# Attention scores in Float32r for three of four batches, a shorter MAX8 for the 32nd score, and batch 1 sent through the first MoE in two groups

## The chip, the cores and the metric

The kernel runs on one core of a Trainium2 chip. The metric is the device time of one execution in microseconds (us). One execution of the kernel before was profiled; its trace has the instructions of TensorE (PE, with its weight loads as PEld), VectorE (DVE), ScalarE (ACT), GpSimd (POOL) and SyncE (SP, which here issues DMAs only), and the DMAs.

## What is computed

Three stages follow each other: attention that keeps the 32 largest scores of each row, a gated MLP ("first MoE", one dense expert), and a layer with 8 experts of which each token uses one ("second MoE").

```python
# q, k, v: 4 batches x 8 heads x 576 rows x 64
scores = scale * np.matmul(q, k.transpose(0, 1, 3, 2))
kth = np.partition(scores, -32, axis=-1)[..., -32:-31]
scores = np.where(scores >= kth, scores, -1e9)
attn = softmax(scores); x = attn @ v            # x: 2304 tokens x 512
x = ((x @ w_a) * (x @ w_b)) @ w_out             # first MoE, d_ff 1536
expert_idx = argmax(x @ w_gate)                 # second MoE, 8 experts
out[mask] = gate_w * (relu(x[mask] @ w1[e]) @ w2[e])
```

## The kernel before

The kernel writes its work as a list of operations, each with an engine, an estimated cost, the tiles that it reads and writes, and a position. A planner (`Plan.emit`) simulates the engines with these costs and fixes the order of each engine's instructions: of the operations that are ready it takes the one with the lowest position. On the chip each engine then runs its list in that order, whatever the real times are. All plain loads and stores go through SP's one queue, in order.

Attention works in units: one batch, one pair of heads. A unit loads q, k and v of the two heads (`load_unit`), and turns q and k with PE transposes, which ACT copies out of PSUM (`prep_unit`). The preparation of a unit is placed in the time of the unit before it. Then come tiles of 128 query rows. Two tiles, the two heads of the same rows, make a pair (kind "N"); the last 64 rows of both heads make one tile (kind "M"). `attn_tiles` computes the scores of a pair in two halves of 288 keys. Each half is two matmuls on float32 operands of 64 partitions (L533; each appears as two instructions in the trace, and so a half as x4). ACT copies the half to SBUF (L537). DVE takes the larger (`m`) and the smaller (`n`) of score j and score j + 288 (L545), finds the 32 largest of `m` by four rounds of MAX8 with three MATCH_REPLACE8 between them (L556, L569, L572), and the 8 largest of `n` by one MAX8 (L575). `attn_kth` makes the 32nd largest score of the row out of these with a minimum over two short lists (L585) and a maximum (L587). `attn_out` masks the exponentials with it (L609 on DVE and L611 on POOL, or L615 on DVE alone), transposes the result (L640), and `attn_av` multiplies by v (L661, L665).

There are 144 tiles, 36 for each batch. `GRP` cuts the 576 tokens of a batch into a group of 320 and one of 256. Of batch 0 the tiles of the first group are computed for all four head pairs, go through the first MoE, and then those of the second (`HALVES` holds 0): 8 units. The batches 1, 2 and 3 have four units each, of 9 tiles, and go through the first MoE with both groups at once.

The first MoE of a batch (`moe1`) runs on PE in float32r, with every operand as a high and a low part and three products (L758 for the two input matrices, L788 for the output matrix). Its matmuls have the lowest priority on PE and fill what attention leaves. For each half of d_ff, six weight pieces of 1 MB (`wt<-ws`) are loaded, each used for all groups at hand, then four of 0.75 MB (`wt<-wos`), through three buffers. A piece that is used for both groups is loaded once for both; batch 0 loads every piece once for each group. The weights come as float64 and are first converted, split and stored to DRAM (`conv`, L369 to L418) in 36 steps, which are placed between the tiles of batch 0 and end with the first tiles of batch 1. After each pass through the first MoE a gating step (`gating`, its first matmul is L871) finds each token's expert and scatters the rows to `xsort`, which is filled with empty rows before by eight DMAs of 771 KB (L339). The second MoE follows when all tokens have been gated.

Of the kernel before, what the change touches and what calls it, by code (L numbers as in the profile page):

```python
# [24 lines left out]
def fr(ap):  # L25
    return ap.bitcast(F32)
# [183 lines left out]
def fused_kernel(ctx: ExitStack, tc: tile.TileContext, q, k, v, w_a, w_b, w_out, w_gate, w1, w2, out,  # L210
# [20 lines left out]
    HALVES = opts.get("halves", (0,))  # L231
# [48 lines left out]
    am_t = [cst.tile([128, S], F32, name="am0")]  # L280
    make_identity(nc, am_t[0][:, 0:128])
    nc.vector.tensor_copy(idr, am_t[0][:, 0:128])
    tri = cst.tile([128, 128], F32, name="tri")
# [21 lines left out]
    rr_t = []  # L305
# [15 lines left out]
    for i in range(1):  # L321
        gb_t.append(cst.tile([128, 346], F32, name=f"gb{i}"))
        nc.gpsimd.memset(gb_t[i], 0.0)
    RR = [P_.fixed(t) for t in rr_t]
# [101 lines left out]
    def load_unit(ui, b, p, groups, pos, after=None):  # L426
        u = Rec()
        u.b, u.p, u.first = b, p, ui == 0
# [9 lines left out]
        for nm, src in (("k", k), ("q", q)):  # L438
            z = T(p_at, [128, 10, 64], F32, "raw" + nm, opts.get("raw", 1))
            u.raw[nm] = z  # L440
            a, e, last = u.c if nm == "q" else (0, 4, True)
            for h in range(2):
                load(c_dma(65536 * (e - a)), pos, lambda z=z, h=h, a=a, e=e: z()[:, h + 2 * a:h + 2 * e - 1:2, :],
                     src[b, h0 + h, 0:512, :].rearrange("(p c) d -> p c d", c=4)[:, a:e], [(z, h)])
            if last:
                load(c_dma(65536), pos, lambda z=z: z()[0:64, 8:10, :],
                     src[b, h0:h0 + 2, 512:576, :].rearrange("h s d -> s h d"), [(z, 2)])
# [9 lines left out]
    def prep_unit(u, i, pos, step):  # L457
        u.rr = RR[i % len(RR)]
        u.qT = T(p_at, [128, 640], F32, "qT", 2)
        u.kT = T(p_at, [128, 640], F32, "kT", 2)  # L460
        for ni, (nm, z) in enumerate((("k", u.kT), ("q", u.qT))):
            raw = u.raw[nm]
            p1 = pos + 3 * ni * step
            a, e, last = u.c if nm == "q" else (0, 4, True)
            t = T(p_ps, [128, 512], F32, "pv", 1) if u.first and nm == "q" else T(p_ps, [128, 1024], F32, "tp", 1)
            cut = [(a, e, last)] if not u.first or nm == "q" else [(0, 2, False), (2, 4, True)]
            for a, e, last in cut:

                o = 128 * e if u.first and nm == "q" else 512

                def tr(t=t, raw=raw, a=a, e=e, last=last, o=o):
                    for c in range(a, e):
                        res = nc.tensor.transpose(t()[:, c * 128:(c + 1) * 128],
                                                  raw()[:, 2 * c:2 * c + 2, :].rearrange("p a d -> p (a d)"), idf)
                    if last:
                        res = nc.tensor.transpose(t()[:, o:o + 64], raw()[0:64, 8:10, :].rearrange("p a d -> p (a d)"),
                                                  idf[0:64, 0:64])
                    return res
                P(PE, 110 * (e - a) + 60 * last, p1, tr, r=[raw], w=[(t, a)], act=0)

                def out(t=t, dst=z, a=a, e=e, last=last, o=o, f=64 * (nm == "k")):
                    if last and f:
                        nc.scalar.copy(dst()[:, 0:64], t()[:, 512:S])
                    if last and 128 * e < 512:
                        nc.scalar.copy(dst()[:, 512:S], t()[:, o:o + 64])
                        last = False
                    x, y = 128 * a, S if last else 128 * e
                    return nc.scalar.copy(dst()[:, f + x:f + y], t()[:, x:y])
                u.mark = P(ACT, c_act(128 * (e - a) + 64 * last) + (150 if last and (e < 4 or nm == "k") else 0), p1,
                           out, r=[(t, a)], w=[(z, a)])  # L490

    def new_group(u, g):
# [3 lines left out]
        r.kth = T(p_sml, [128, 5], F32, "kth", 2)  # L496
# [6 lines left out]
    def attn_tiles(lst, r, pos):  # L503
# [8 lines left out]
        if kind == "M":  # L512
            sp = T(p_ps, [128, 2, 512], F32, "sp", 1)

            def score():
                for hh, hf in ((0, 0), (1, 1), (0, 1), (1, 0)):
                    a = slice(64 * hh, 64 * hh + 64)
                    res = nc.tensor.matmul(sp()[a, hf, 0:HS], u.qT()[a, 512:576], u.kT()[a, 64 + hf * HS:64 + (hf + 1) * HS],
                                           start=True, stop=True)
                return res  # L520
            P(PE, 980, pos, score, r=[u.qT, u.kT], w=[sp], label=f"score{u.b}")
# [3 lines left out]
        else:  # L525
            for hf in range(2):
                sp = T(p_ps, [128, 2, 512], F32, "sp", 1)

                def score(hf=hf, sp=sp):
                    for h in range(2):  # L530

                        a, k0 = slice(64 * h, 64 * h + 64), 0 if h else 64
                        res = nc.tensor.matmul(sp()[:, h, 0:HS], u.qT()[a, c * 128:(c + 1) * 128],  # L533
                                               u.kT()[a, k0 + hf * HS:k0 + (hf + 1) * HS], start=True, stop=True)
                    return res
                P(PE, 510, pos, score, r=[u.qT, u.kT], w=[sp], label=f"score{u.b}")
# [30 lines left out]
        for x in range(1, 4):  # L567
            for h, (i, j, kind, _, c) in enumerate(lst):
# [5 lines left out]
                if x == 1:  # L574
                    P(DVE, c_dve(HS), pos + 5.0 * h + 0.5, lambda h=h, j=j: nc.vector.max(  # L575
                        out=kt(j, 40, 48), in_=n()[:, h]), r=[(n, h)], w=[KT(j, 5)])
        return res

    def attn_kth(r, j0, j1, pos):
        def kt(a, b):  # L580
            return r.kt()[:, j0:j1, a:b]

        def KT(x):
# [936 lines left out]
```

## Time and profile before

| | |
|---|---|
| median of 3 runs | 1248.7 us (1246.32 to 1249.34) |
| the profiled execution | 1250.73 us, its span 1248.9 us |
| mean granted PE clock | 0.944 of full speed |
| PE busy | 1136.4 us, 91% of the span |
| DVE busy | 893.8 us, 72% |
| ACT busy | 741.5 us, 59% |
| POOL busy | 539.2 us, 43% |
| DMA | 208.01 MB, mean 167 GB/s |

The shares are means over stages with different limits: attention and the first MoE overlap, and the second MoE comes alone at the end. A matmul's busy time is longer than the step from one matmul to the next, since matmuls are pipelined, so that costs of PE are read as steps between start times.

### The profile page before, as it was taken

The numbers are of one execution on the slowest core, as the hardware profiler recorded it, in microseconds if no ns is written. First come the engines' busy times: TensorE is split into PE (matmuls) and PEld (weight loads), VectorE is DVE, ScalarE is ACT, GpSimd is POOL, SyncE is SP. The second block draws the span as 40 slices with busy tenths as digits, with TensorE's granted clock in tenths as the row PEclk, the third lists the DMA queues.
The fourth block names the chain that finished last, engine by engine and source line by source line (L and its number), as shares of the span: only waits on it lengthen the run. The fifth ranks groups of instructions, "written<-read, shape, count | busy, mean of one in ns | idle before, by whom it ended". The sixth has DMA issues, their size and how long they took to land.

```text
span 1248.9 us, 22260 instructions
## 1 busy us (share of the span) xinstructions
PE 1136.4 (91%) x7614; PEld 950.9 (76%) x7614; DVE 893.8 (72%) x2574; ACT 741.5 (59%) x1639; POOL 539.2 (43%) x673
## 2 busy tenths in 40 slices
PE   5666587987999999999999999999899999999997
PEld 2333365675687878878878777899899889999996
DVE  6999989999989999989999898901004644444451
ACT  6767677777677776656766665633223545544451
POOL 4766667577554744324544532555334110000011
PEclk9966588898899999999999999999999999999999
DMA  7486566898466554243243322345545645554550
GB/s 232 137 275 186 164 178 188 288 327 264 161 208 200 188 183 131 77 130 131 77 137 100 113 86 104 119 140 202 196 167 179 200 151 171 181 175 145 166 180 28
DMA packets 133375, 208.01 MB, mean 167 GB/s; under 512 B 53075, under 2 KB 95059, under 8 KB 125573
## 3 DMA queue, kind: packets, MB, share of 16 engines
q1 hardware_dynamic: 130037, 197.04, 48.5%
q0 software_dynamic: 3216, 9.46, 2.0%
q8 instruction: 62, 1.02, 0.3%
q14 instruction: 60, 0.49, 0.1%
HBM read 171.82 MB, written 35.25 MB: 166 GB/s over the span
## 4 chain that ended last, share of the span: by engine, by line
PE 62%; DVE 20%; issue 7%; DMA 5%; ACT 3%; POOL 2%; SPq 1%; POOLq 0%; ACTq 0%; DVEq 0%
PE ab L758 20%; PE ab L788 11%; PE sp L533 5%; PE ab L1116 5%; DVE m L569 4%; PE pv L661 4%; DVE kt L572 4%; PE tp L640 3%; PE ms L1165 3%; PE pv L1165 3%; DVE am L609 2%; DVE kt L556 1%; DMA xsort<-rows,pi 1%; DVE am L615 1%; DVE m L545 1%
## 5 line engine op out<-in xcount | busy, mean ns | idle before, releaser
L758 PE MATMUL ab<-xh,wt 128*128 128x320 f32 (+1 forms) x1344 | 311.1, 309 | 3.4 <-ACT sb L743 3.4
L758 PEld LDWEIGHTS ab<-xh,wt 128*128 128x128 f32 x1344 | 228.3, 192 | 30.3 <-issue 22.6
L758 PE MATMUL ab<-xl,wt 128*128 128x320 f32 (+1 forms) x672 | 200.4, 298 | 0.0
L569 DVE MATCH_REPLACE8 m<-kt,m 128x288 f32<-128x288 f32 x432 | 190.6, 447 | 0.0
L572 DVE MAX8 kt<-m 128x8 f32<-128x288 f32 x432 | 184.8, 452 | 0.7
L788 PE MATMUL ab<-gH,wt 128*128 128x320 f32 (+1 forms) x768 | 172.0, 307 | 2.8 <-DMA wt<-wos 2.8
L533 PE MATMUL sp<-kT,qT 64*128 64x288 f32 x512 | 111.2, 514 | 40.5 <-ACT s L537 13.0
L766 POOL TENSOR_TENSOR sa<-sa,sb 128x320 f32<-128x320 f32 (+1 forms) x96 | 80.2, 836 | 149.2 <-ACT sb L743 145.6
L788 PEld LDWEIGHTS ab<-gH,wt 128*128 128x128 f32 x768 | 129.8, 193 | 14.9 <-issue 10.1
L611 POOL TENSOR_TENSOR am<-am,e 128x576 f32<-128x576 f32 x78 | 119.1, 1532 | 31.8 <-DVE am L609 25.7
L758 PEld LDWEIGHTS ab<-xl,wt 128*128 128x128 f32 x672 | 129.2, 192 | 0.0
L1190 POOL DMA_INDIRECT out_dram<-y,ti x23 | 23.0, 999 | 228.0 <-ACT y L1184 213.3
L564 ACT ACTIVATE e<-s,nm 128x576 f32<-128x576 f32 x144 | 109.5, 777 | 16.4 <-POOL nm L559 15.5
L788 PE MATMUL ab<-gT,wt 128*128 128x320 f32 (+1 forms) x384 | 114.8, 299 | 0.0
L640 PE MATMUL tp<-idr,am 128*128 128x128 f32 x512 | 87.9, 307 | 24.7 <-DVE am L615 12.3
L1034 DVE TENSOR_TENSOR wp<-raw,wp 128x1024 fp32r<-128x1024 f32 (+1 forms) x73 | 67.5, 943 | 55.0 <-ACT wp L1033 52.6
L537 ACT COPY s<-sp 128x576 f32<-128x576 f32 x128 | 81.8, 639 | 41.9 <-PE sp L533 31.0
L395 POOL TENSOR_TENSOR gT<-sa,gH 128x320 fp32r<-128x320 f32 (+1 forms) x96 | 82.6, 861 | 39.5 <-ACT gH L394 38.1
L640 PEld LDWEIGHTS tp<-idr,am 128*128 128x128 f32 x512 | 65.7, 157 | 44.4 <-POOL am L611 14.4
L533 PEld LDWEIGHTS sp<-kT,qT 64*128 64x128 f32 x512 | 44.1, 209 | 72.3 <-issue 28.2
L1116 PE MATMUL ab<-xgh,wp 128*128 128x304 f32 (+6 forms) x352 | 89.5, 312 | 1.2 <-DVE gT L1123 0.7
L644 ACT COPY aT<-tp 128x512 f32<-128x512 f32 x128 | 73.4, 586 | 24.6 <-PE tp L640 23.7
(286 smaller groups left out, 2559.6 us busy)
## 6 DMA issues: line engine op xcount, KB each, us to landing
wt<-ws SPq DMA_DIRECT2D x54, 1024.0 KB, 4.8
wt<-wos SPq DMA_DIRECT2D x44, 768.0 KB, 4.6
raw<-in_moe_w_dram SPq DMA_DIRECT2D x64, 512.0 KB, 3.5
xsort<-rows SPq DMA_DIRECT2D x8, 771.0 KB, 10.5
wp<-ws SPq DMA_DIRECT2D x6, 1024.0 KB
rawk<-in_k_dram SPq DMA_DIRECT2D x40, 128.0 KB, 3.6
vt<-in_v_dram SPq DMA_DIRECT2D x20, 256.0 KB, 4.4
gT<-in_moe_w_a_dram SPq DMA_DIRECT2D x8, 512.0 KB
```

The costliest lines, as they stand in the source:

```text
L395: P(POOL, c_pool(cost), pos, lambda: nc.gpsimd.tensor_sub(lo(), src(), fr(hi())), r=rd + wh, w=wl)
L533: res = nc.tensor.matmul(sp()[:, h, 0:HS], u.qT()[a, c * 128:(c + 1) * 128], u.kT()[a, k0 + hf * HS:k0 + (hf + 1) * HS], start=True, stop= ...
L537: P(ACT, c_act(S), pos, lambda hf=hf, sp=sp: nc.scalar.copy(s()[:, :, hf * HS:(hf + 1) * HS], sp()[:, :, 0:HS]), r=[sp], w=[(s, (h, hf)) f ...
L564: P(ACT, c_act(S, True) + 90, pos, lambda h=h, e=e: nc.scalar.activation(e(), s()[:, h], AF.Exp, bias=nm()[:, h], scale=SCALE), r=[(s, (h, ...
L569: P(DVE, c_dve(HS), pos + 5.0 * h, lambda x=x, h=h, j=j: nc.vector.match_replace(out=m()[:, h], in_to_replace=kt(j, 8 * x - 8, 8 * x), in_ ...
L572: P(DVE, c_dve(HS), pos + 5.0 * h, lambda x=x, h=h, j=j: nc.vector.max(out=kt(j, 8 * x, 8 * x + 8), in_=m()[:, h]), r=[(m, h)], w=[KT(j, x)])
L611: P(POOL, c_pool(S), pos, lambda: nc.gpsimd.tensor_mul(am(), am(), e()), r=[e], w=[amk])
L640: res = nc.tensor.transpose(tp()[:, 512 * h + x * 128:512 * h + (x + 1) * 128], z()[:, 640 * h + x * 128:640 * h + (x + 1) * 128], idf)
L758: res = nc.tensor.matmul(pa()[:, 0:n], view()[:, m, wi, ko, :], xv()[:, ko], start=(ko == 0 and x == 0), stop=(ko == KO - 1 and x == 2))
L766: P(POOL, c_pool(n), pos, lambda: nc.gpsimd.tensor_mul(sa()[:, 0:n], sa()[:, 0:n], sb()[:, 0:n]), r=[sb], w=[sa])
L788: res = nc.tensor.matmul(pa()[:, 0:n], wv()[:, wi, f, :], gv()[:, f, :], start=(f == 0 and x == 0), stop=(f == HB - 1 and x == 2))
L1116: res = nc.tensor.matmul(pa()[:, 0:cap], p1[ko]()[:, wi, f * 128:(f + 1) * 128], xv()[:, ko], start=(ko == 0 and i == 0), stop=(ko == KO - ...
```

## The change

1. `HALVES` becomes (0, 1): batch 1 too is computed group by group. It then has 8 units and goes through the first MoE in two passes, with its weight pieces loaded twice and a gating step after each. There are 24 units instead of 20, still with 144 tiles.
2. `FU` is the set of units that keep float32 scores: the first eight, which are those of batch 0. For all others q and k are split into a high and a low float32r part (`hl`: a copy on ACT, a subtraction on POOL), transposed with both parts stacked on 128 partitions, and copied out for each head. For k a second copy with the two parts exchanged (`kS`) is made by two DMAs on SP's queue. A half of a pair's scores is then four float32r matmuls with 128 partitions: q's stack times `kT` and times `kS`, for each head. The rows of kind "M" use eight. q, k and v are loaded whole for each such unit. The planner's cost of a float32 half goes from 510 to 780 ns; that of a float32r half is 490.
3. The 32nd score: the last round of MAX8 on `m` (8 values) and the MAX8 on `n` (8 values) lie side by side, and one MAX8 over these 16 values for each tile replaces L585 and L587. Its 8th value is the 32nd score.
4. The small last transposes of an "M" tile (L624, 64 by 64) become one of 128 by 128 on a tile padded with zeros.

```diff
-    HALVES = opts.get("halves", (0,))
+    HALVES = opts.get("halves", (0, 1))
+    FU = opts.get("fu", range(8))
...
-        u.b, u.p, u.first = b, p, ui == 0
+        u.b, u.p, u.f, u.first = b, p, ui in FU, ui == 0
...
+            load(c_dma(262144), pos, lambda z=z: z()[:, 0:8, :].rearrange("p (h c) d -> p h c d", h=2),
+                 src[b, h0:h0 + 2, 0:512, :].rearrange("h (p c) d -> p h c d", c=4), [(z, 0)])
             for h in range(2):
...
+                load(c_dma(16384), pos, lambda z=z, h=h: z()[64 * h:64 * h + 64, 8, :], src[b, h0 + h, 512:576, :],
+                     [(z, 1 + h)])
...
+        u.qT = T(p_at, [128, 2, 512], F32R, "qT", 2)
+        u.kT = T(p_at, [128, 2, 640], F32R, "kT", 2)
...
+        u.kS = T(p_at, [128, 2, 640], F32R, "kS", opts.get("kS", 2))
+        for ni, nm in enumerate(("k", "q")):
             raw = u.raw[nm]
...
+            p0 = pos + 3 * ni * step
+            hl = T(p_at, [128, 9, 2, 64], F32R, "hl", opts.get("hl", 1))
+            P(ACT, c_act(576, True), p0, lambda raw=raw, hl=hl: nc.scalar.copy(hl()[:, :, 0, :], raw()[:, 0:9, :]),
+              r=[raw], w=[(hl, 0)])
+            P(POOL, c_pool(576), p0, lambda raw=raw, hl=hl: nc.gpsimd.tensor_sub(
+                hl()[:, :, 1, :], raw()[:, 0:9, :], fr(hl()[:, :, 0, :])), r=[raw, (hl, 0)], w=[(hl, 1)])
+            for h in range(2):
+                p1 = p0 + step * (1 + h)
+                t = T(p_ps, [128, 1024], F32R, "tp", 1)
+                lst = [(c, 4 * h + c) for c in range(4)] + ([(4, 8)] if h else [])
+
+                def tr(t=t, lst=lst, hl=hl):
+                    for c, j in lst:
+                        r = nc.tensor.transpose(t()[:, c * 128:(c + 1) * 128],
+                                                hl()[:, j].rearrange("p a d -> p (a d)"), idr)
+                    return r
+                P(PE, 56 * len(lst), p1, tr, r=[hl], w=[t], act=0)
+                if nm == "q":
+                    P(ACT, c_act(512), p1, lambda t=t, h=h: nc.scalar.copy(u.qT()[:, h, :], fr(t()[:, 0:512])),
+                      r=[t], w=[(u.qT, h)])
+                else:
+                    P(ACT, c_act(512), p1, lambda t=t, h=h: nc.scalar.copy(u.kT()[:, h, 64:576], fr(t()[:, 0:512])),
+                      r=[t], w=[(u.kT, h)])
...
+                    for a in range(2):
+                        u.mark = P(SP, c_dma(294912), p1, lambda a=a: nc.sync.dma_start(
+                            fr(u.kS()[64 * a:64 * a + 64]).rearrange("p h c -> p (h c)")[:, 64:],
+                            fr(u.kT()[64 - 64 * a:128 - 64 * a]).rearrange("p h c -> p (h c)")[:, 64:]),
+                          r=[u.kT], w=[(u.kS, a)])
...
+                        for x, kk in enumerate((u.kT(), u.kS())):
+                            res = nc.tensor.matmul(sp()[:, h, 0:HS], u.qT()[:, h, c * 128:(c + 1) * 128], kk[:, h, kc],
+                                                   start=(x == 0), stop=(x == 1))
                     return res
-                P(PE, 510, pos, score, r=[u.qT, u.kT], w=[sp], label=f"score{u.b}")
+                P(PE, 780 if u.f else c_mm(HS, 4), pos, score, r=[u.qT, u.kT] + ([] if u.f else [u.kS]), w=[sp],
+                  label=f"score{u.b}")
...
-                        out=kt(j, 40, 48), in_=n()[:, h]), r=[(n, h)], w=[KT(j, 5)])
+                        out=kt(j, 32, 40), in_=n()[:, h]), r=[(n, h)], w=[KT(j, 4)])
...
-        P(DVE, 77 + 8 * (j1 - j0 - 1), pos, lambda: nc.vector.tensor_tensor(
-            kt(32, 40), r.kt()[:, j0:j1, 30:22:-1], kt(40, 48), op=OP.min), r=KT(2) + KT(3) + KT(5), w=KT(4))
-        P(DVE, 78 + 9 * (j1 - j0 - 1), pos, lambda: nc.vector.tensor_reduce(
-            r.kth()[:, j0:j1], kt(31, 40), axis=AX.X, op=OP.max), r=KT(3) + KT(4), w=[(r.kth, j) for j in range(j0, j1)])
...
+        for j in range(j0, j1):
+            P(DVE, 80, pos, lambda j=j: nc.vector.max(out=r.kt()[:, j, 40:48], in_=r.kt()[:, j, 24:40]),
+              r=[(r.kt, (j, 3)), (r.kt, (j, 4))], w=[(r.kt, (j, 5))])
```

The branch for the units in `FU` is the old code of `load_unit` and `prep_unit`, moved into an `if u.f`.

## Rows read from the trace of the kernel before

**Rows 1.** Busy time by stretch; after POOL: granted PE clock, DMA share, GB/s.

```profile
225.00:350.00 125.00, 110.53 (x682) 83.24 (x680) 119.30 (x354) 90.99 (x207) 76.89 (x85) 0.92 0.79 254
350.00:430.00 80.00, 79.34 (x605) 64.46 (x603) 73.14 (x247) 61.00 (x149) 46.51 (x63) 1.00 0.60 200
430.00:640.00 210.00, 209.82 (x1509) 169.56 (x1510) 193.14 (x627) 140.04 (x322) 97.06 (x131) 1.00 0.38 123
640.00:811.00 171.00, 169.44 (x1216) 136.97 (x1215) 153.53 (x506) 109.02 (x252) 71.64 (x103) 1.00 0.31 107
811.00:975.00 164.00, 158.03 (x1187) 153.84 (x1185) 22.24 (x79) 55.74 (x146) 70.62 (x100) 0.99 0.52 181
```

**Rows 2.** The same view, one stretch of 25 us in the early stage.

```profile
275.00:300.00 25.00, 20.46 (x120) 15.81 (x122) 23.92 (x73) 20.39 (x49) 19.17 (x22) 0.88 0.99 317
```

**Rows 3.** Timeline of SP's issues: start, length, what, count.

```profile
303.87 0.53 SPq L418 DMA_DIRECT2D wos<-gH  x1
...
334.65 3.06 SPq L736 DMA_DIRECT2D wt<-ws  x2
```

**Rows 4.** Chain that ended last, in order of time: start, length, what.

```profile
243.44 1.88 PE pv L661 x16
...
437.73 1.88 PE pv L661 x16
...
805.46 0.44 PE tp L640 x4
...
816.55 1.62 PE ab L758 x12
...
825.50 19.20 PE ab L788 x144
844.69 0.68 PE ms L871 x8
```

**Rows 5.** Timeline of PE: a preparation of k, then an "M" score.

```profile
440.12 0.66 PE L473 MATMUL tp<-idr,rawk 128*128 128x128 f32 x4
...
440.90 1.19 PE L518 MATMUL sp<-kT,qT 64*64 64x288 f32 x8
```

**Rows 6.** Timeline of PE: a score half between two other pieces.

```profile
449.47 0.31 PE L758 MATMUL ab<-xh,wt 128*128 128x320 f32 x1
449.71 0.76 PE L533 MATMUL sp<-kT,qT 64*128 64x288 f32 x4
450.40 0.44 PE L882 MATMUL ms<-idr,rows 128*128 128x128 f32 x2
```

**Rows 7.** Groups by line and shape: busy us, mean ns, idle before.

```profile
L611 POOL TENSOR_TENSOR am<-am,e 128x576 f32<-128x576 f32 x78 | 119.1, 1532 | 31.8 <-DVE am L609 25.7 <-PE sp L518 2.9 <-PE sp L533 2.2
...
L644 ACT COPY aT<-tp 128x512 f32<-128x512 f32 x128 | 73.4, 586 | 24.6 <-PE tp L640 23.7
...
L575 DVE MAX8 kt<-n 128x8 f32<-128x288 f32 x144 | 65.3, 453 | 0.0
...
L585 DVE TENSOR_TENSOR kt<-kt 128x16 f32<-128x16 f32 x64 | 21.3, 334 | 0.1
...
L488 ACT COPY kT<-tp 128x576 f32<-128x576 f32 x19 | 12.3, 648 | 0.0
...
L587 DVE TENSOR_REDUCE kth<-kt 128x2 f32<-128x18 f32 x64 | 10.3, 161 | 0.1
```

**Rows 8.** One line's instructions: shortest, median, longest ns, first and last start.

```profile
L585 DVE TENSOR_TENSOR kt<-kt x80: 144/176/1296, 21.8 to 809.0; 128x16 f32<-128x16 f32 x64, 128x8 f32<-128x8 f32 x16
...
L575 DVE MAX8 kt<-n x144: 435/452/482, 15.5 to 807.6; 128x8 f32<-128x288 f32 x144
...
L615 DVE SCALAR_TENSOR_TENSOR am<-s,kth,e x66: 794/814/1902, 31.0 to 810.7; 128x576 f32<-128x576 f32 x66
```

**Rows 9.** Waits of SP's queue: us in total, times, longest.

```profile
SPq L776 <- PE ab L758: 170.2, 21, 16.2
```

**Rows 10.** The page, DMA issues: count, KB each, us to landing.

```profile
xsort<-rows SPq DMA_DIRECT2D x8, 771.0 KB, 10.5
```

More of the change, by code (lines that the diff above doesn't have):

```diff
@@ L304, in fused_kernel @@
     nc.gpsimd.memset(wg, 0.0)
-    rr_t = []
+    qm_t, rr_t = [], []
+    for i in range(2):
+        qm_t.append(cst.tile([128, 192], F32R, name=f"qm{i}"))
+        nc.gpsimd.memset(fr(qm_t[i]), 0.0)
     for i in range(opts.get("rr", 1)):
@@ L323, in fused_kernel @@
         nc.gpsimd.memset(gb_t[i], 0.0)
+    QM = [P_.fixed(t) for t in qm_t]
     RR = [P_.fixed(t) for t in rr_t]
@@ L457, in prep_unit @@
     def prep_unit(u, i, pos, step):
[L458 to L461, printed above, removed]
-            raw = u.raw[nm]
[L463 to L490, printed above, removed]
@@ new lines, in prep_unit, with tr, out @@
+        u.qm, u.rr = QM[i % 2], RR[i % len(RR)]
+        u.qT = T(p_at, [128, 2, 512], F32R, "qT", 2)
+        u.kT = T(p_at, [128, 2, 640], F32R, "kT", 2)
+        if u.f:
+            u.qv, u.kv = (lambda z=z: fr(z()).rearrange("p h c -> p (h c)")[:, 0:640] for z in (u.qT, u.kT))
+            for ni, (nm, z, dst) in enumerate((("k", u.kT, u.kv), ("q", u.qT, u.qv))):
+                raw = u.raw[nm]
+                p1 = pos + 3 * ni * step
+                a, e, last = u.c if nm == "q" else (0, 4, True)
+                t = T(p_ps, [128, 512], F32, "pv", 1) if u.first and nm == "q" else T(p_ps, [128, 1024], F32, "tp", 1)
+                cut = [(a, e, last)] if not u.first or nm == "q" else [(0, 2, False), (2, 4, True)]
+                for a, e, last in cut:
+                    o = 128 * e if u.first and nm == "q" else 512
+                    def tr(t=t, raw=raw, a=a, e=e, last=last, o=o):
+                        for c in range(a, e):
+                            res = nc.tensor.transpose(t()[:, c * 128:(c + 1) * 128],
+                                                      raw()[:, 2 * c:2 * c + 2, :].rearrange("p a d -> p (a d)"), idf)
+                        if last:
+                            res = nc.tensor.transpose(t()[:, o:o + 64], raw()[0:64, 8:10, :].rearrange("p a d -> p (a d)"),
+                                                      idf[0:64, 0:64])
+                        return res
+                    P(PE, 110 * (e - a) + 60 * last, p1, tr, r=[raw], w=[(t, a)], act=0)
+                    def out(t=t, dst=dst, a=a, e=e, last=last, o=o, f=64 * (nm == "k")):
+                        if last and f:
+                            nc.scalar.copy(dst()[:, 0:64], t()[:, 512:S])
+                        if last and 128 * e < 512:
+                            nc.scalar.copy(dst()[:, 512:S], t()[:, o:o + 64])
+                            last = False
+                        x, y = 128 * a, S if last else 128 * e
+                        return nc.scalar.copy(dst()[:, f + x:f + y], t()[:, x:y])
+                    u.mark = P(ACT, c_act(128 * (e - a) + 64 * last) + (150 if last and (e < 4 or nm == "k") else 0), p1,
+                               out, r=[(t, a)], w=[(z, a)])
+            return
@@ L515, in score @@
             def score():
[L516 to L519, printed above, removed]
-                return res
-            P(PE, 980, pos, score, r=[u.qT, u.kT], w=[sp], label=f"score{u.b}")
+                if u.f:
+                    for hh, hf in ((0, 0), (1, 1), (0, 1), (1, 0)):
+                        a = slice(64 * hh, 64 * hh + 64)
+                        res = nc.tensor.matmul(sp()[a, hf, 0:HS], u.qv()[a, 512:576],
+                                               u.kv()[a, 64 + hf * HS:64 + (hf + 1) * HS], start=True, stop=True)
+                    return res
+                for hf in range(2):
+                    for hh in range(2):
+                        for kk in (u.kT(), u.kS()):
+                            res = nc.tensor.matmul(sp()[:, hf, 0:HS], u.qm()[:, 64 * hh:64 * hh + 128],
+                                                   kk[:, hh, 64 + hf * HS:64 + (hf + 1) * HS],
+                                                   start=(hh == 0 and kk is u.kT()), stop=(hh == 1 and kk is u.kS()))
+                return res
+            P(PE, 980 if u.f else c_mm(HS, 8), pos, score, r=[u.qT, u.kT] if u.f else [u.qm, u.kT, u.kS], w=[sp],
+              label=f"score{u.b}")
             P(ACT, c_act(S), pos, lambda: nc.scalar.copy(
```

57 lines of the change are left out of this document (34 added, 23 removed).

## Prediction

> **What bounds the kernel now.** I read the busy times by stretch first, because the page's shares mix stages. In each row the reader is to compare PE with the length of the stretch. From 225 to 350 us PE works 110.5 of 125 us at a mean clock of 0.92, while DVE is busy 119.3; from 350 to 811 it works 458.6 of 461 us at full clock [rows 1]. So PE is the limit from about 340 us on, and DVE, with 92% there, comes close behind. After 811 us DVE is nearly idle and PE goes on with the first MoE.
>
> Second comes the queue of SP, for where the early stage ends. The last converted piece of the output weights is stored at 303.87 us, and the first weights of batch 0's second group are issued at 334.65 [rows 3]. Until then PE waits for conversions, which DVE, ACT, POOL and the DMAs share with attention; between 275 and 300 us the DMAs are busy 0.99 of the time [rows 2].
>
> Third, the chain that ended last shows what slack attention has. Its last piece ends at 816.55 us; PE then still has batch 2's first MoE to finish, whose gating starts at 844.69 [rows 4]. Batch 3's first MoE begins behind it. So attention may end some 28 us later without harm, and time is saved by shortening PE's list after 340 us, not by shortening DVE's.
>
> **Scores.** A float32 half takes PE 0.80 us: the last matmul before it starts at 449.47, the next would start 0.133 later (144 float32r matmuls of 320 and 256 columns in 19.20 us [rows 4]), and the instruction behind the half starts at 450.40 [rows 6]. Four float32r matmuls of 288 columns, the mean of those two widths, with the same 128 by 128 weights, take 4 x 0.133 = 0.53. The gain is 0.27 for a half; if the gap of about 0.11 us before it stays, it is 0.16. There are 3 batches x 4 head pairs x 4 tile pairs x 2 halves = 96, so 25.6 us, at least 15. An "M" score takes 1.19 us now [rows 5] and 8 x 0.133 = 1.07 then: nothing to speak of.
>
> **Preparation on PE.** k takes 440.90 - 440.12 = 0.78 us [rows 5], q as much, 12 units: 18.7 us. Then it is 18 transposes for each of 16 units, 288 in all. No row has a float32r transpose. Its floor is the 128/288 of 0.133 by columns, 0.06 us; its ceiling the float32 one, 0.44/4 = 0.11 [rows 4]. That gives 17 to 32 us; I take 0.08 for the weight load behind each, 23 us, so +4 (between -2 and +13).
>
> **What of it counts.** PE's list gets 26 - 4 = 22 us shorter (2 to 28). Batch 1's attention runs from 243 to 438 us [rows 4], so half of its 32 halves lie ahead of 340, where PE waits anyway: 4 us of gain is lost there and 2 us of the added transposes are free. A second gating for batch 1 costs PE about 1 us (its first matmuls take 0.68 [rows 4]). Some -19 us remain. The larger transposes of the "M" tile change a fifth of a microsecond 16 times at most, and both ways.
>
> **The 32nd score.** For a pair DVE drops 334 + 161 ns and adds two MAX8 over 16 values. MAX8 over 288 takes 453 [rows 7]; over 16 it lies between nothing and that; nearest in size is the reduction of 18 values, 161. So 495 becomes about 320, on 64 pairs 11 us, at worst a loss of 26. It is DVE time beside PE's full list: after 340 us it is worth nothing, ahead of it, where DVE paces the conversions, 25 pairs x 0.175 = 4 us, of which I count 3.
>
> L585 shows why it is dear: 144 ns at the shortest, 176 median, 1296 at the longest, while MAX8 stays between 435 and 482 [rows 8]. The Trainium skill, "SBUF — State Buffer", section "Who interferes with whom", says that a VectorE instruction with two SBUF inputs and a GpSimd instruction that reads SBUF shut each other out for a whole instruction, and one with a single input does not. The trace agrees, with the spreads just named. By that rule the change takes L585 out of POOL's way, but its 32 new POOL subtractions come in the way of L615 (814 median, 1902 longest [rows 8]); at the price of the wait that L615 has now, for POOL time that grows by a seventh, this gives back some 2 us of DVE, and the sum stays.
>
> **ACT, POOL and DMA.** A unit's ACT work is now two copies of 576 at 0.65 us [rows 7] and one small one, 1.5 us; then two copies of 576 from SBUF (0.65), four of 512 at 0.59 [rows 7], and four small ones at half of that: 4.8. So 16 x 4.8 - 12 x 1.5 = 59 us more on ACT, which is busy 401 of the 586 us from 225 to 811 [rows 1], so 68% becomes 78%. POOL gets 32 subtractions of 576 at 1.5 us [rows 7], 49 us, from 50% to 58%. Neither is a limit by its share. But PE's results wait for ACT in two buffers, each filled again in 12 x 0.133 = 1.6 us, hardly longer than two or three ACT copies in a row. PE stands still 2.4 of the 461 us now; I add 3 us, between 0 and 15.
>
> The second loading of batch 1's weights adds 12 + 6 = 18 MB between 340 and 660 us, where the DMAs are busy 0.4 to 0.6 of the time. Batch 0's second group, loaded in the same one-group way, lets PE work 79.3 of 80 us at 200 GB/s [rows 1]. I cost it at nothing; the cover is that DMA room, and without it each piece would hold PE for the part of 1 MB / 317 GB/s = 3.3 us [rows 2] that exceeds its matmuls (24 x 0.133 = 3.2). Ahead of 340 us there is no room: batch 1 begins two units more in that stretch, each with 0.9 MB from DRAM and 0.6 MB of `kS`, 3 MB or 9 us of full DMAs. If the last conversions stand behind this, PE's full stretch begins up to 9 us later; I take 4, so with DVE's gain of 3 the stretch begins 1 us later.
>
> The split itself gives PE little, since at 340 us it already has a full list; it makes batch 1's first group ready before batch 0's second is through, and so covers the seam at about 445 us.
>
> **Sum.** -19 + 1 + 3 = -15; I keep 2 us more for waits that I have not found, -13. The profiled execution took 1250.7 us, 2.0 more than the median of the runs: 1237.7 there, 1236 for the median.
>
> **Rivals.**
>
> *Late scores (slower).* `kS` is issued on SP, in order, behind weight loads that wait for a free buffer, 21 times, up to 16.2 us [rows 9], and a DMA in the full stretch took 10.5 us to land [rows 10]. Scores wait for it, and DVE for them. For it: a chain of copy, subtraction, transposes, copies and two DMAs where before there were transposes and a copy. Against it: preparation runs a unit ahead, 40 us in batches 2 and 3, though only some 20 in batch 1. Attention has 28 us of slack, less PE's gain of 15, plus DVE's 7 after 340: 20. From a stretch of 20 + 13 = 33 us on, 2 us for each of 16 units, the change loses; at 3 us for each unit it is 48, so 28 past the slack, and 1236 + 28 = 1264.
>
> *ACT becomes the limit of PE's buffers (no change).* At 15 us of waits instead of 3, and transposes at 0.11 (+9 more), the sum is about +8 less 1: 1236 + 12 to 1236 + 20, 1248 to 1256; with one of the two, 1245 to 1248.
>
> *The early stage is filled (a larger gain).* From 225 to 350 us PE loses 14.5 us idle and 8% of clock on the rest, 23 in all [rows 1]. A plan with truer costs may start the full stretch earlier by most of that: 1236 - 17 = 1219. Against it: the conversions still set the stage.
>
> **Chances.** A difference under 0.3%, 4 us, can't be told from none. Forecast (1227 to 1245): 0.50; larger gain: 0.10; no change: 0.16; late scores: 0.24. The no-change case reaches a little over both of its bounds. Faster 0.62, within 0.3% 0.15, slower 0.23. The likeliest case's own range is 1227 to 1245; that for 8 in 10 reaches into the others: 1219 to 1262.
>
> **What would show it.** Right: float32r score halves of about 0.53 us between neighbours on PE; PE full from about 340 us; the gating of batch 2 some 15 us earlier than 844.69; attention's end before 816 us. DVE's new MAX8 near 160 ns with little spread. Wrong: transposes at 0.11 us or more; PE idle behind ACT's copies in the first MoE; DVE waiting for scores at the start of units and the second weights issued well after 334.65; attention ending after the first MoE of batch 2.

## The result: 1.2% slower

| | before | after |
|---|---|---|
| median us (four runs each) | 1247.9 (1246.32 to 1249.34) | 1263.49 (1262.62 to 1263.57) |
| the profiled execution, its span | 1250.73, 1248.9 | 1262.62, 1260.7 |
| mean granted PE clock | 0.944 | 0.939 |
| DMA | 208.0 MB | 240.4 MB |

The ratio is 1.012, 95% interval 1.0105 to 1.0135. The forecast was 1236. The time, and the late attention, are those of the rival "late scores" (1264).

Page of after, busy time of each engine:

```profile
PE 1116.9 (89%) x7790; PEld 990.0 (79%) x7790; DVE 897.8 (71%) x2570; ACT 782.0 (62%) x1764; POOL 578.2 (46%) x707
```

PE is busy 19.5 us less, and the kernel still takes longer. The busy time by stretch (columns as in [rows 1]) says where PE stood still instead:

```profile
225.00:350.00 125.00, 101.50 (x711) 90.09 (x711) 98.29 (x295) 92.81 (x222) 83.74 (x93) 0.92 0.89 286
350.00:430.00 80.00, 74.81 (x594) 67.46 (x591) 57.07 (x185) 59.58 (x146) 48.69 (x61) 0.96 0.77 244
430.00:640.00 210.00, 202.53 (x1560) 183.98 (x1558) 192.33 (x612) 153.75 (x369) 115.47 (x148) 1.00 0.69 226
640.00:811.00 171.00, 162.71 (x1205) 146.41 (x1206) 166.29 (x539) 117.41 (x279) 72.17 (x99) 0.97 0.34 111
```

Against [rows 1], PE's idle time grows from 14.5 to 23.5 us in the first stretch, from 0.7 to 5.2 in the second, from 0.2 to 7.5 in the third and from 1.6 to 8.3 in the fourth: 27.5 us together. The granted clock falls with it: 1.00 from 350 to 811 us before, 0.96 and 0.97 in the second and fourth stretch after. There it drops to the lower of its two levels (1.2 GHz) for a few us at a time, where PE has stood still: from 360 to 370 us PE is busy 7.04 us at a mean clock of 0.67, and 2.9 us of its idle time are in one piece. So a part of PE's busy time in after is work at half the clock. DVE, which sets the pace of attention, is busy 98 us of the first stretch instead of 119, and 57 of the second instead of 73. The DMA share rises from 0.79 to 0.89, from 0.60 to 0.77 and from 0.38 to 0.69.

Waits of DVE in after while batch 1's attention runs (242 to 477 us; us in total, times, longest):

```profile
DVE m L614 <- ACT s L606: 29.2, 9, 8.3
DVE sum L752 <- POOL sum L750: 14.1, 5, 3.5
DVE m L614 <- PE sp L601: 9.3, 3, 7.4
```

The same view of before, from 243 to 440 us:

```profile
DVE m L545 <- ACT s L537: 4.2, 3, 1.6
DVE n L545 <- ACT s L537: 2.5, 4, 0.7
DVE sum L686 <- POOL sum L684: 1.7, 3, 0.8
...
DVE m L545 <- PE sp L533: 1.0, 2, 0.6
```

DVE now waits 12 times, 38.5 us, for the first scores of a pair (5 times, 5.2 us, before), and 14.1 us for sums from POOL (1.7 before). One such wait, timeline of DVE in after (the bracket is the idle time ahead and what ended it):

```profile
307.50 0.19 DVE L752 RECIPROCAL sum<-sum 128x5 f32<-128x5 f32 x1 [3.06 <-POOL sum L750]
316.00 0.76 DVE L614 TENSOR_TENSOR m<-sp,s 128x576 f32<-128x576 f32 x1 [8.31 <-ACT s L606]
```

The chain that ended last, in after, leads to this wait through two transfers:

```profile
274.27 13.61 DMA xsort<-rows
...
293.10 10.26 DMA wt<-wos
303.40 1.97 PE ab L854 x6
...
316.00 0.76 DVE m L614
```

By this chain the scores that DVE waits for stand in PE's list behind matmuls of the first MoE (L854), which start when a weight piece (`wt<-wos`) has landed, and SP issues that piece only after a fill of `xsort` and the loads of a unit. Just ahead of 303 us PE also stands idle 3.3 and 3.4 us for POOL.

So batch 1's attention takes 236 us (its last product with v starts at 477 us) where it took 194 [rows 4]: 42 us more for the same 36 tiles. Batches 2 and 3 win back some of it. PE timeline of after, the ends that answer to 816.55 and 844.69 in [rows 4]:

```profile
641.42 0.64 PE L937 MATMUL ms<-x,wg 128*32 128x256 f32 x8
...
842.39 1.95 PE L727 MATMUL pv<-aT,vt 128*64 128x256 f32 x16
...
854.85 0.75 PE L937 MATMUL ms<-x,wg 128*32 128x320 f32 x8
```

The gating of batch 1's last tokens starts at 641, where before it was 657: there PE's gain is still seen. But that lead is the first MoE's alone, taken while attention fell behind: attention ends at 842 instead of 814 (start of the last product), and batch 2's gating comes at 855 instead of 845. The balance of PE closes: -19.5 of busy time, +20.8 of idle time from 225 to 640 us, +6.7 from 640 to 811 and +3.8 elsewhere make the +11.8 us of the two profiled spans (the medians differ by 15.6).

### The profile page after: what moved, and what is told of

Its sections match the earlier page's. It is cut to its first block, busy times and chain, and to the rows that moved or that the text cites. A ratio compares the mean times of both kernels' runs of the same rounds, so it can differ in the third digit from the quotient of the medians.

```text
span 1260.7 us, 23056 instructions
## 1 busy us (share of the span) xinstructions
PE 1116.9 (89%) x7790; PEld 990.0 (79%) x7790; DVE 897.8 (71%) x2570; ACT 782.0 (62%) x1764; POOL 578.2 (46%) x707
## 4 chain that ended last, share of the span: by engine, by line
PE 45%; DVE 23%; issue 10%; DMA 10%; ACT 6%; POOL 4%; SPq 2%; POOLq 0%; DVEq 0%; ACTq 0%
PE ab L824 13%; PE ab L854 8%; DVE m L638 5%; PE ab L1182 5%; DVE kt L641 4%; PE pv L727 3%; PE sp L601 3%; PE pv L1231 2%; PE tp L706 2%; PE ms L1231 2%; DMA xsort<-rows,pi 2%; DMA wt<-wos 2%; DVE am L674 2%; DVE am L680 2%; DVE kt L625 1%
## 5 line engine op out<-in xcount | busy, mean ns | idle before, releaser
L824 PE MATMUL ab<-xh,wt 128*128 128x320 f32 (+1 forms) x1344 | 307.7, 306 | 6.7 <-ACT sb L809 3.5
L854 PE MATMUL ab<-gH,wt 128*128 128x320 f32 (+1 forms) x768 | 176.9, 308 | 8.0 <-DMA wt<-wos 4.5
L641 DVE MAX8 kt<-m 128x8 f32<-128x288 f32 x432 | 181.9, 443 | 0.4
L676 POOL TENSOR_TENSOR am<-am,e 128x576 f32<-128x576 f32 x78 | 122.2, 1571 | 75.2 <-DVE am L674 42.8
L854 PEld LDWEIGHTS ab<-gH,wt 128*128 128x128 f32 x768 | 133.0, 195 | 10.7 <-DMA wt<-wos 4.3
L854 PE MATMUL ab<-gT,wt 128*128 128x320 f32 (+1 forms) x384 | 115.9, 302 | 0.0
L706 PE MATMUL tp<-idr,am 128*128 128x128 f32 x512 | 80.6, 296 | 13.6 <-DVE am L680 4.4
L706 PEld LDWEIGHTS tp<-idr,am 128*128 128x128 f32 x512 | 62.8, 152 | 27.6 <-issue 6.8
L727 PE MATMUL pv<-aT,vt 128*64 128x320 f32 (+1 forms) x512 | 80.0, 446 | 4.7 <-ACT aT L695 4.1
L597 PE MATMUL sp<-kT,qT 64*128 64x288 f32 x128 | 36.4, 656 | 51.2 <-DVE n L614 21.1
```

The lines of the kernel that those rows point to most:

```text
L641: P(DVE, c_dve(HS), pos + 5.0 * h, lambda x=x, h=h, j=j: nc.vector.max(out=kt(j, 8 * x, 8 * x + 8), in_=m()[:, h]), r=[(m, h)], w=[KT(j, x)])
L676: P(POOL, c_pool(S), pos, lambda: nc.gpsimd.tensor_mul(am(), am(), e()), r=[e], w=[amk])
L706: res = nc.tensor.transpose(tp()[:, 512 * h + x * 128:512 * h + (x + 1) * 128], z()[:, 640 * h + x * 128:640 * h + (x + 1) * 128], idf)
L727: nc.tensor.matmul(pv()[64 * h:64 * h + 64, 0:n], u.vt()[:, h, j, :], r.aT[h]()[:, j, 0:n], start=(j == 0), stop=False)
L824: res = nc.tensor.matmul(pa()[:, 0:n], view()[:, m, wi, ko, :], xv()[:, ko], start=(ko == 0 and x == 0), stop=(ko == KO - 1 and x == 2))
L854: res = nc.tensor.matmul(pa()[:, 0:n], wv()[:, wi, f, :], gv()[:, f, :], start=(f == 0 and x == 0), stop=(f == HB - 1 and x == 2))
```

## The experiments

Each ran beside the kernel before on the same chip; the ratio is to that. The ends are the starts of the last products with v in the profiled execution.

| kernel | units, float32r in | us | ratio (95%) | batch 1's attention ends | attention ends |
|---|---|---|---|---|---|
| e3_max8_only | 20, none | 1237.83 | 0.9909 (0.9890 to 0.9927) | 427 | 787 |
| e2_split_f32 | 24, none | 1248.65 | 0.9995 (0.9981 to 1.0009) | 426 | 786 |
| e4_split_f32r_23 | 24, batches 2, 3 | 1230.91 | 0.9851 (0.9835 to 0.9867) | 425 | 798 |
| e14_f32r_half1 | 24, and half of batch 1 | 1244.46 | 0.9964 (0.9940 to 0.9989) | 454 | 826 |
| (after) | 24, batches 1, 2, 3 | 1263.49 | 1.0120 (1.0105 to 1.0135) | 477 | 842 |
| e5_nosplit_f32r_23 | 20, batches 2, 3 | 1221.94 | 0.9780 (0.9764 to 0.9797) | 420 | 788 |
| e16_nosplit_f32r_10 | 20, and half of batch 1 | 1224.26 | 0.9823 (0.9779 to 0.9868) | 424 | 797 |
| e1_nosplit | 20, batches 1, 2, 3 | 1245.95 | 0.9968 (0.9949 to 0.9987) | 443 | 803 |
| e11_max8_510 | e3, the planner's old cost | 1241.07 | 0.9920 (0.9904 to 0.9936) | 436 | 810 |

### One part at a time

The two switches, here as e3 sets them (e2: only `FU`, 24 units; e1: only `HALVES`; e4 and e5: `range(16)` and `range(12)`, so that batches 2 and 3 alone have float32r):

```diff
-    HALVES = opts.get("halves", (0, 1))
-    FU = opts.get("fu", range(8))
+    HALVES = opts.get("halves", (0,))
+    FU = opts.get("fu", range(24))
```

e1_nosplit: 

> Float32r scores and the short MAX8, batch 1 unsplit (four units of 9 tiles, both groups through the first MoE at once). Theory A (the loop of preparation, from the raw load of k over the kS transfer's landing to the next raw load, takes 27 to 42 us in batch 1 and is longer than a unit of 5 tiles, some 24 us, but not longer than one of 9 tiles, some 49 us; the delay needs the split and float32r together): the score waits of VectorE in batch 1 fall from 35 us to under 15 and the time to 1230 to 1240 us. Rival B (float32r preparation alone costs it, by its load on ScalarE, GpSimd and the DMAs): 1255 to 1265 us. Rival C (the split alone costs it): as A for this run, 1230 to 1240.

e2_split_f32: 

> Batch 1 split and the short MAX8, float32 scores in all batches. Theory A: no stall, since the float32 preparation has no kS transfer: 1243 to 1250 us, about the kernel before. Rival B: the same. Rival C (the split alone costs it, by the second loading of weights and of q, k, v): 1258 us or more.

e3_max8_only: 

> The short MAX8 alone (with the truer planner cost of float32 scores and the padded transposes of the M tiles), float32 scores, batch 1 unsplit. All three theories: within 5 us of the kernel before, 1243 to 1250 us. If it is slower by 10 us or more, the delay comes from the MAX8 or from the new order of the plan, and A, B and C all fall.

e4_split_f32r_23: 

> Batch 1 split with float32 scores, float32r scores in batches 2 and 3 only. Theory A: batch 1 is not delayed, and two thirds of the float32r gain on TensorE stay, all behind 340 us: 1230 to 1240 us. Rival B: a smaller delay in batches 2 and 3, 1248 to 1258. Rival C: 1250 to 1260, the price of the split less the gain of float32r.

e5_nosplit_f32r_23: 

> Short MAX8, batch 1 unsplit with float32 scores, float32r scores in batches 2 and 3 only. If the effects add (float32r in batches 2 and 3 gave 18 us beside the split, the MAX8 alone 11): 1237.8 - 17.7 = 1220 us, 1216 to 1226. If the split is what lets TensorE use the gain (its list runs dry at the end of batch 1 without it): 1228 to 1238, no better than the same with the split, 1231.

The rows of the table make a ladder. MAX8 alone (e3, with the planner's costs and the padded transposes) is worth -11 us. Splitting batch 1 on top (e2) costs 11. Float32r in batches 2 and 3 (e4 against e2) brings 18, and float32r in batch 1 (after against e4) costs 33. -11 + 11 - 18 + 33 = +15; that this is near the measured +15.6 is no test, since each step starts where the one before ended. Without the split it is -16 for batches 2 and 3 (e5 against e3) and +24 for batch 1 (e1 against e5). Float32r in batch 1 does most of the harm. The split does the rest: 9 to 11 where batch 1 has float32 (e4 against e5, e2 against e3), and 17.5 where it has float32r (after against e1). e5 leaves both out and is the fastest kernel of the study, 2.2% faster than before.

Where MAX8's 11 us come from, SP's issues in e3: the last converted pieces, and the first weights of batch 0's second group:

```profile
277.22 1.99 SPq L424 DMA_DIRECT2D wos<-gH  x2
308.42 23.19 SPq L802 DMA_DIRECT2D wt<-ws  x5
```

In [rows 3] these stand at 303.87 and 334.65. DVE's work in batch 0 gets 5.5 us shorter (20 calls of L585 and 20 of L587 took 10.4 us up to 243 us, 36 of the new MAX8 take 4.9), and the end of the early stage moves forward by 26. That the one causes all of the other is argued: e3 also holds the padded transposes and a new order of the plan. Batch 0's attention ends at 235 instead of 243, the first gating comes at 324 instead of 345.

e11 undoes the planner's cost in e3:

```diff
-                P(PE, 780 if u.f else c_mm(HS, 4), pos, ...
+                P(PE, 510 if u.f else c_mm(HS, 4), pos, ...
```

> The short MAX8 alone again (batch 1 unsplit, float32 scores), with the planner's old cost of 510 ns for a float32 score half. If the 11 us came from the MAX8: 1235 to 1242 us. If they came from the truer cost in the plan: 1245 to 1250.

The truer cost accounts for 1.4 of the 11 us by the ratios and 3.2 by the medians; the intervals of e3 and e11 overlap, so it may be nothing.

### Which half of batch 1

e14 is after with `range(12)` (batch 1's first group in float32), e16 is without the split, with `range(10)`.

e14_f32r_half1: 

> Batch 1 split; its first group (units 9 to 12, beside the conversions and the fills) with float32 scores, its second group and batches 2 and 3 with float32r and kS. If the early stage is what makes the float32r preparation dear (rival G): 1224 to 1236 us, as with float32 in all of batch 1 (1231) or a little less. If the short units of 5 and 4 tiles are (theory A's units): about half of the 32 us that float32r in batch 1 cost, 1243 to 1252.

e16_nosplit_f32r_10: 

> Batch 1 unsplit, float32r from its third unit on (two of its four units, behind the conversions). By rival G: 1216 to 1224 us, as with float32 in all of batch 1 (1222) or a little less. If float32r costs in batch 1 wherever it stands, or TensorE's list runs dry at its end: 1228 to 1240.

Without the split, the last two units of batch 1 cost 2.3 us and the first two 22: the harm lies in the early stage. With the split the second group costs 13.5 and the first 19: its units are half as long and so twice as often prepared, which is the likely reason; no run tests it.

### What holds the scores back

Edits to after, each by itself: in e6 the next unit's loads are placed behind the last copy into `kT`, no longer behind the transfer of `kS`; in e13 q and k are loaded into two buffers instead of one, in e8 v into three instead of two.

```diff
 e6                  P(ACT, ...)                  # last copy into kT
-                    P(ACT, ...
+                    u.mark = P(ACT, ...
-                        u.mark = P(SP, c_dma(294912), p1, ...   # kS
+                        P(SP, c_dma(294912), p1, ...
 e13
-opts.get("raw", 1)
+opts.get("raw", 2)
 e8
-"vt", opts.get("vt", 2)
+"vt", opts.get("vt", 3)
```

e6_mark: 

> The changed kernel, with one edit to the plan: the next unit's loads are put behind the last copy of kT and no longer behind the kS transfer. Theory A (the loop of preparation, whose last link is kS landing before the next raw loads are issued): the loads of batch 1 are issued some 5 to 10 us earlier and the time falls to 1245 to 1256 us. Rival D (each unit's own chain, copy, subtraction, transposes, copies, kS on a full DMA, is late by itself): under 4 us of gain, 1259 to 1264. Rival E (SyncE's queue stands behind loads of v that wait for the end of an earlier unit's attention): the same, 1259 to 1264.

e8_vt3: 

> The changed kernel with three buffers for v instead of two, so that a load of v waits for a unit's attention one unit further back. Rival E: SyncE's wait for the attention products in batch 1 (35 us) falls under 10 and the time to 1240 to 1254. Theory A and rivals D and F: 1259 to 1264.

e13_raw2: 

> The changed kernel with two buffers each for the raw q and k, so that a unit's loads need not wait for the unit before. If the loop of preparation through its single raw buffers holds batch 1: 1240 to 1254 us. If the full DMAs and queues of the early stage hold it: 1258 to 1266.

They took 1259.82 (0.3% faster than after), 1266.86 and 1261.88 us, with batch 1 done at 482, 484 and 479. None is the cause. The intervals of e8 and e13 overlap that of after; e6 gains some 4 us, so an order of the plan is worth about that much. The idea behind e1's first theory, a loop of loads and preparation that is longer than a short unit, falls with e6 and e13.

e7 drops the transfer of `kS` and multiplies by `kT` twice; e9 makes the transfer, but no score reads it. Both so leave the products of high and low parts out of the scores of batches 1 to 3. e7 also places the next unit's loads as e6 does.

```diff
 e7
-                    for a in range(2):
-                        u.mark = P(SP, ... nc.sync.dma_start(kS <- kT) ...
 e7 and e9
-                        for x, kk in enumerate((u.kT(), u.kS())):
+                        for x in range(2):        # kT both times
```

e7_no_kS: 

> The changed kernel without the kS transfer: the second matmul of each pair repeats the first, so the cross products of high and low parts are left out of the scores of batches 1 to 3, and TensorE's instructions stay as many and as wide. Theory A and rival D (the transfer and its landing on full DMAs delay batch 1): the score waits of VectorE in batch 1 fall under 15 us and the time to 1226 to 1240. Rival E: little change, 1255 to 1264. Rival F (the load of the float32r preparation on ScalarE and GpSimd, or the wider loads of q and k): 1250 to 1264.

e9_kS_unread: 

> The changed kernel with the kS transfers issued as before, but read by nobody: the second matmul repeats the first, so the cross products of high and low parts are left out of the scores of batches 1 to 3. If the scores' wait for the transfer's landing is the cause (rival D): 1228 to 1240 us, as without the transfer (1232). If the transfer's traffic or its place in SyncE's queue is the cause: 1252 to 1264.

e7 took 1232.17 us (0.9872, 0.9853 to 0.9891), e9 1267.88 (1.0134, 1.0117 to 1.0152). The first stretch in e7, then in e9:

```profile
225.00:350.00 125.00, 104.16 (x739) 90.33 (x738) 112.14 (x325) 99.54 (x239) 88.59 (x96) 0.97 0.79 267
```

```profile
225.00:350.00 125.00, 102.33 (x709) 91.33 (x708) 98.72 (x288) 92.84 (x217) 82.08 (x89) 0.90 0.88 281
```

This is the sharpest pair. The transfer is worth 31 us (some 28 when e6's placing of the loads is taken off), and it costs as much when nobody waits for its data. So it harms by being issued and carried, not by being late. DVE's waits from 225 to 480 us go with it: for copied scores (`m` after ACT's `s`) 29.2 us in after, 19.3 in e9, 4.8 in e7 and 0.9 in e4, for sums from POOL 15.6, 18.4, 8.0 and 6.4. The profile of after says the same of PE: the tile `kS`, "its engine sat idle before it until", us and times, and below it the landing times:

```profile
  DMA kS<-kT: 0.7, 1
...
DMA to landing us min/median/max: 3.2/6.3/12.8
```

PE waited 0.7 us for `kS` in the whole run.

e15 puts the suspected cost where it is missing: into e4, whose batch 1 has float32 scores, two unread transfers within SBUF for each unit of batch 1, 295 KB each. e18 issues the same transfers at the same places with 8 KB.

```diff
+                if nm == "k" and u.b == 1:
+                    dk = T(p_at, [128, 2, 640], F32R, "kS", 2)
+                    for a in range(2):
+                        P(SP, ..., nc.sync.dma_start(fr(dk()[:, a, 0:576]), u.kv()[:, 0:576]), ...)   # e18: 0:16
```

e15_f32_plus_dma: 

> Batch 1 split with float32 scores, float32r in batches 2 and 3 (1231 us), and in each unit of batch 1 two transfers within SBUF of 295 KB behind the copies of k, as large as those of kS and read by nobody. If the transfers' traffic and their place in SyncE's queue cost the time: 1245 to 1260 us. If not: 1228 to 1236.

e18_f32_tiny_dma: 

> As the run with float32 in batch 1 and two added transfers for each of its units, but each of 8 KB instead of 295 KB (16 columns instead of 576). If the place in the queue costs the time: 1242 to 1252 us, near the 1249.5 of the large ones. If the traffic does: 1229 to 1236, near the 1231 without.

1249.53 us (e15) and 1238.91 (e18) against e4's 1230.91: 8 us for 16 more places in SP's queue, 10.6 for what they carry, 18.6 together; a part of the 8 may be the plan's new order. So transfers that nobody reads can cost that much here. But the 18.6 aren't a share of the 33, since they come about in another way. In e15 the early stage ends later: the first weights of batch 0's second group are issued at 333 us, in e4 at 315, and batch 1's attention ends at 432, 7 us after e4's. In after those weights come at 313, and it is batch 1's attention that is late, by 52 us against e4.

Last, another carrier of `kS`: ACT copies between partitions, for batch 1 (e10; e12 without the split), or the same DMAs issued from ACT's queue (e17).

```diff
 e10, e12 (batch 1)
-                        u.mark = P(SP, ... nc.sync.dma_start(kS <- kT) ...
+                        u.mark = P(ACT, ... nc.scalar.copy(kS <- kT) ...
 e17
-                        u.mark = P(SP, ... nc.sync.dma_start(kS <- kT) ...
+                        u.mark = P(ACT, ... nc.scalar.dma_start(kS <- kT) ...
```

e10_kS_act: 

> The changed kernel, with kS made in batch 1 by two ScalarE copies of 64 partitions x 1216 from kT instead of two DMAs; the full result. If the DMA's latency in batch 1 is the cause: 1228 to 1242 us, though 8 units x 2.4 us go to ScalarE. If ScalarE's load in batch 1 is near its limit: 1245 to 1262.

e12_nosplit_kS_act: 

> Batch 1 unsplit, float32r scores in batches 1 to 3, with batch 1's kS by ScalarE as in the run with the split; the full result. If the transfer's latency in batch 1 is all that the unsplit float32r version (1246) lost against the one with float32 in batch 1 (1222): 1214 to 1224 us. If TensorE's list runs dry before batch 1's attention ends, as it did there between 423 and 443 us: 1226 to 1240.

e17_kS_actq: 

> The changed kernel with the kS transfers issued from ScalarE's DMA queue instead of SyncE's; same traffic, full result. If the transfers' place in SyncE's in-order queue (it stands still until kT is copied, with the loads behind it) is what costs: 1236 to 1252 us. If their traffic beside the full DMAs is: 1257 to 1268.

1272.66, 1240.84 and 1278.20 us. With short units ACT copies are worse than the transfer (+9, against after), with long ones better (-5, against e1). A copy on ACT in e10 (mean ns behind the busy time), then its first stretch:

```profile
L543 ACT CAST kS<-kT 64x1216 fp32r<-64x1216 f32 x16 | 19.3, 1207 | 0.3
```

```profile
225.00:350.00 125.00, 105.57 (x756) 92.67 (x755) 101.47 (x304) 102.79 (x235) 85.65 (x95) 0.96 0.80 273
```

The DMA share is back at 0.80, but ACT is now busy 103 of 125 us and DVE still only 101. That ACT has no room there either is the likely reading. e17 came out above both of its ranges and doesn't tell the place in SP's queue from the traffic: it puts the issues, 0.5 to 2.5 us each in batch 1, into ACT's list, and in it the early stage is late as well (first weights of batch 0's second group at 333 us).

Of the expectations, e1 fell between its ranges and e18 too; e3, e8, e9, e10, e12, e16 and e17 fell outside, e12 and e16 by less than 1 us.

## Why the prediction was wrong, point by point

**Scores and preparation: right.** Timeline of PE in after:

```profile
251.40 0.29 PE L601 MATMUL sp<-kT,qT 128*128 128x288 f32 x1
251.53 0.29 PE L601 MATMUL sp<-kS,qT 128*128 128x288 f32 x1
251.66 0.30 PE L601 MATMUL sp<-kT,qT 128*128 128x288 f32 x1
251.80 0.30 PE L601 MATMUL sp<-kS,qT 128*128 128x288 f32 x1
251.93 0.55 PE L523 MATMUL tp<-idr,hl 128*128 128x128 f32 x5
252.32 0.38 PE L824 MATMUL ab<-xh,wt 128*128 128x320 f32 x1
```

A half takes 251.93 - 251.40 = 0.53 us, the five transposes 0.39, so 0.078 each; the forecast had 0.53 and 0.08. PE's list got 19.5 us shorter by busy time, which holds the time at the lower clock, where 22 by steps were forecast. Two readings are off without weight: DVE's share from 350 to 811 us is 91% by [rows 1], not 92, and POOL's 49 us are a sixth of its 292, not a seventh.

**What of it counts: right for batches 2 and 3.** The forecast's two thirds of 26 - 4 are some 15 us; measured, 16 and 18.

**The 32nd score: the duration right, its worth mis-sized.** One of the new instructions, all 144 (shortest, median, longest ns):

```profile
L652 DVE MAX8 kt<-kt x144: 147/160/180, 21.0 to 838.3; 128x8 f32<-128x16 f32 x144
```

Two of these are the forecast's 320 ns a pair. But the removed L585 was not alike everywhere. By shape, before, from 0 to 243 us (busy us, mean ns):

```profile
L585 DVE TENSOR_TENSOR kt<-kt 128x16 f32<-128x16 f32 x16 | 6.6, 410 | 0.0
```

From 440 to 820 us it is 270, so the saving is largest early. The forecast counted 25 pairs ahead of 340 us, batch 0's 16 and some 9 of batch 1, each at the mean of the whole run, which gave 4 us, "of which I count 3". Batch 0 alone saves 5.5, and the time falls by 9 to 11: the price of an early us was the larger error. The Trainium skill's "SBUF — State Buffer", section "Who interferes with whom", holds here. Counted instruction by instruction, of the 80 L585 before 33 ran beside an elementwise instruction of POOL, with a mean of 502 ns, and 47 without one, with a mean of 169; the new MAX8, of one input, has a mean of 163 ns beside POOL and 161 without. The rule's other side was cheap, as taken: L680 (L615 before) has a mean of 1043 ns for 979, 4 us over 66.

**The split: failed.** "I cost it at nothing" is 9 to 11 us, and 17.5 beside float32r in batch 1. The second loading is not what the cover was short of: in e2 8 of the 11 us are there at the first gating (332 us, 324 in e3), before any weight of batch 1 is loaded. What is different by then is batch 1's first units, half as long, each with its own loads and preparation. How the 11 divide among these was not measured. The seam that the split should cover at about 445 us isn't there before: PE is busy 45.00 of the 45 us from 415 to 460. It is there in e1, with 8.3 us idle, and smaller in after, with 2.7.

**ACT, POOL and DMA: the step that failed.** It says "Ahead of 340 us there is no room" and "I take 4", the +1 of the sum when DVE's gain is taken off. The place was right; float32r in batch 1, PE's gain included, costs 24 us without the split and 33 with it. And it was looked for in the wrong thing. "If the last conversions stand behind this" asks about the conversions, but in after their last stores and the first weights of batch 0's second group are issued earlier than in [rows 3]:

```profile
287.94 1.49 SPq L424 DMA_DIRECT2D wos<-gH  x2
...
313.47 0.38 SPq L802 DMA_DIRECT2D wt<-ws  x1
```

Without the split the last store does come later with float32r in batch 1, at 291 us in e1 and 279 in e5, but the first weights only by 5 us (314 and 309). What comes late is batch 1's attention, which has its first units in the same stretch. DVE falls to 98 of 125 us. The loads by engine were priced high: ACT has 40.5 us more to do, not 59, and POOL 39, not 49.

**Late scores: the outcome right, the mechanism wrong.** Scores did come late (48 us priced in all, 42 measured in batch 1). But "Scores wait for it" fell: with `kS` unread nothing is gained. By e7 and e9 the issue and traffic of the transfer delay other things. Which ones is argued; SP's in-order loads are among the candidates. SP's issues in after:

```profile
266.51 6.55 SPq L424 DMA_DIRECT2D wos<-xl  x2
273.11 1.11 SPq L440 DMA_DIRECT2D rawk<-in_k_dram  x1
274.27 5.63 SPq L345 DMA_DIRECT2D xsort<-rows  x1
279.95 4.73 SPq L440 DMA_DIRECT2D rawk<-in_k_dram  x2
```

With the DMAs full, one issue takes up to 5.6 us, and the loads of the next unit's k are spread over 11 us. Long issues alone aren't the cause: in e4, 2.6% faster than after, one of `xsort<-rows` takes 9.5 us at 264 us. And between 270 and 303 us the chain of e9 goes through ACT, DVE, POOL and PE, not through transfers, so the path isn't the same even in after and e9, which are equally slow.

**The slack: failed.** "Attention may end some 28 us later without harm", 20 after the other edits, was read at the end of attention only. Of the added idle time of PE, 20.8 us lie before 640: PE then lacks attention's matmuls and, the likely reading, the tokens of batch 1 for the first MoE as well. PE's gain of 19.5 us is gone there, before the slack at the end comes into play. And no lateness behind 816 us was free: among the split kernels with float32r in all or half of batch 1, attention's end at 816 us goes with 1232 (e7), 826 with 1244 (e14), 842 with 1263 (after), 848 with 1268 (e9), 853 with 1273 (e10), about 1.1 us for each us from 816 on; e6, e8, e13 and e17 lie within 6 us of that line. Ahead of 816 it may be otherwise: e4 ends at 798 with 1231, about e7's time, but its list on PE is longer. That two numbers go together doesn't show that the end of attention sets the time. The 1264 of "late scores" came out right by luck, by two errors that cancel: 48 us of lateness less 20 of slack, where the runs show 28 of lateness at the end and no slack behind 816.

**Open.** In e7, without `kS`, batch 1 still takes 213 us against e4's 190, and the kernel is 1.3% faster than before all the same, likely because its list on PE is shorter and the MAX8 acts early. How that divides among ACT's added copies, POOL's subtractions and the larger loads wasn't separated; nor which delayed transfer costs most of `kS`'s 31 us.

## What to carry to other kernels

A conversion that makes PE faster paid here only where PE was the limit: apply it by stage, and keep the old form in the units that run beside a full set of DMAs. Cost an added transfer by what its issue and traffic take from all others in its stage, not only by who waits for its data: to leave it in place unread, and to add it unread elsewhere, are two cheap tests of this. Whether the unread copy costs by the same path as the transfer that you suspect is to be read from its trace: here it didn't. A saving on the engine that sets the pace of an early stage can be worth more than its own us, 9 to 11 for 5.5 in batch 0 here.

## What the runs showed of the hardware

SBUF to SBUF transfers of 295 KB, two for each of 8 short units and read by nobody, cost 18.6 us in this kernel, of which 8 remain at 8 KB each (e15, e18 against e4). Those of `kS` took 3.2 us to land at the shortest, 6.3 at the median and 12.8 at the longest, over the whole run of after. A two-input VectorE instruction over 16 values has a mean of 410 ns in one stage and 270 in another of the same kernel, beside a shortest of 144; beside an elementwise instruction of POOL it has 502, without one 169. A MAX8 over as many stays within 147 and 180.
